# Moving loads, two kv products and the transposes of batch 1 in a fused attention and gated-MLP kernel

## The chip, the cores and the metric

The kernel runs on one core of one Trainium2 chip. The metric is the device time of one execution in microseconds (us). One profiled execution leaves a trace; its span is about 1.8 us shorter than the time of the same execution (285.1 us against 286.9), and span differences equal time differences. The time of one kernel is not one number: 50 runs of the kernel before, over all series, have mean 286.80 us, standard deviation 0.27 us and range 286.39 to 287.32. Effects of a few tenths of a microsecond are read from the trace, and the times only confirm sums.

Ratios are the mean time of one kernel's runs over that of the other's of the same rounds, so not quite the ratio of the medians quoted. An interval is a 95% interval.

## The reference

```python
# q, k, v: (8 batches, 8 heads, 576 tokens, 64), float32
q_s = softmax(q, axis=-1)            # over the 64 of a head
k_s = softmax(k, axis=2)             # over the 576 tokens
kv  = einsum('bhsd,bhse->bhde', k_s, v)
x   = einsum('bhsd,bhde->bhse', q_s, kv)     # -> (4608 tokens, 512)
h   = x @ w_in                        # 512 x 2048
g   = h * sigmoid(beta * h)
out = g @ w_out                       # 2048 x 512
```

## The kernel before

The 4608 tokens are worked in nine slabs `t` of 512 (eight batches, and a ninth slab for the 64 tokens that each batch has over 512, its "remainder"). A slab has two passes of 64 matmuls of 128x512: pass 1 (XT times w_in, then SiLU on ScalarE) and pass 2 (times w_out). The attention of batch t+1 or t+2 is threaded between those matmuls. Heads go in pairs, 0 to 3. For one pair: exp of q on ScalarE, normalization on VectorE or GpSimd, four 128x128 transposes on TensorE; exp of k, nine 65-column matmuls (kv), a scaling of kv on VectorE ("kvd"), one 512-column product that gives the pair's part of XT, and a copy of that from PSUM to SBUF.

A scheduler of its own places them: `(slot, step)`, where the slot counts matmuls of the slab. For slab 0, slots 64 to 128 are pass 2, in which all of batch 1's attention must happen.

```python
def spread(steps, lo, hi):
    return [(lo + (hi - lo) * k / len(steps), s) for k, s in enumerate(steps)]

TT = (116, 128)
...                                    # w_in in five column chunks, cast to bf16 on arrival
for m in (0, 2):
    load_win(0, m, 2)
for c in range(1, len(WCH)):
    load_win(c)
...
for c in range(4):
    load_wout(c)                       # into the same staging buffers
...
# slab 0: what is threaded between the matmuls
todo = [(TT[k_], lambda k_=k_: go(t_steps(1, (2 * k_, 2 * k_ + 1), (1 + k_,)))) for k_ in range(2)]
todo += [(113, lambda: o2_evac(0, 0, 3, ACTE)), (114, lambda: o2_evac(0, 1, 4, ACTE))]
todo.append((114.5, lambda: (exp_kh(1, 2, 2, 0), exp_kh(1, 2, 2, 1))))
todo.append((110, lambda: (norm_main(1, 2, 1), norm_main(1, 3, 1))))
todo += spread(kv_steps(1, (0, 1), (0,)), 121, 122.5)
todo += [(127.5, lambda: (out_now(1, 0, 7, DVE), out_now(1, 1, 1, ACTE)))]
...
for c in range(4):
    scale_wout(c)                      # VectorE: w_out / beta, to bf16
load_main("qf", qt_h, QF, 1, 4)        # batch 1's queries
for cs in ((0, 1), (2, 3)):
    load_k(1, 4, cs)
    load_v(1, 4, cs)
```

Nearly all loads are issued from SyncE's queue, in program order.

The softmax here doesn't subtract the row's maximum and nothing guards it: scores larger than these inputs give would overflow.

Of the kernel before, what the change touches and what calls it, by code (L numbers as in the profile page):

```python
# [158 lines left out]
def bass_efficient_attn_shen__then__act_swish_beta_kernel(  # L159
# [12 lines left out]
    with ExitStack() as es:  # L172
# [74 lines left out]
        def load_main(name, th, bufs, b, split=1, cs=None, engs=(SP,)):  # L247
            i = b % 2
            n = H // split
            for c in cs or range(split):  # L250
                add(engs[c % len(engs)], lambda e, c=c: e.dma_start(dst(bufs[i], c * n, n), src(th, b, c * n, n)),  # L251
                    w=[(name, i, hp) for hp in range(c * n // 2, (c + 1) * n // 2)],
                    slot=f"{name}{i}_{c}")
# [23 lines left out]
        def load(b):  # L277
# [5 lines left out]


        load_main("qf", qt_h, QF, 0, 4, None, (SP, ACTE))
        add(ACTE, lambda e: e.activation(DUMMY[:, 0:1], WARM[:, 0:1], ACT.Exp), r=["warm"],
            w=["dummy"])

# [195 lines left out]
            return s  # L484

        def attn_late(b):
            s = spread(kv_steps(b, (0, 1)), 99, 103) + spread(kv_steps(b, (2, 3)), 105, 109)
            x = []
            for hp in range(NHP):
                x += out_step(b, hp, MB)  # L490
            return s + spread(x, 110, 123)

        def spread(steps, lo, hi):
            return [(lo + (hi - lo) * k / len(steps), s) for k, s in enumerate(steps)]
# [31 lines left out]
        def out_now(b, hp, bk, eng):  # L526
            i = b % 2
            out_mm(b, hp, bk)
            add(eng, lambda e: (e.copy if eng == ACTE else e.tensor_copy)(
                XT[i][:, hp, :], PS[bk][:, :]),  # L530
                r=[("ps", bk)], w=[("xt", i, hp)], bank=[bk])
# [13 lines left out]
                s()  # L545


        for i, n in enumerate((2, 4)):
            a = bass.AP(beta_h, FG[n][0], [[128 * n, len(FG[n])], [1, 128 * n]])
            add(SP, lambda e, i=i, a=a: e.dma_start(BT[i][:, :], a), w=[("bt", i)],  # L550
                slot=f"bt{i}")
        load_k(0, 4)
        load_v(0, 4)

# [20 lines left out]
        def wkeys(c, m, nm):  # L575
            if c == 0:
                return [("wst", 0, h) for h in range(m // 2, (m + nm + 1) // 2)]
            return SKEY[0][2:] if c == 1 else SKEY[c - 1]

        def load_win(c, m=0, nm=NM):  # L580
            c0, n = WCH[c]
            a = bass.AP(win_h, m * 128 * DFF + c0, [[DFF, 128], [128 * DFF, nm], [1, n]])
            s = STAGE[c0 // 512][:, m:m + nm, c0 % 512:c0 % 512 + n]
            add(SP, lambda e: e.dma_start(s, a), w=wkeys(c, m, nm), slot=f"win{c}{m}")  # L584
# [54 lines left out]
        norm_main(0, 3, 1)  # L639
        go(t_steps(0, (1,), HEAD))  # L640
        warm(1, 0, True)
        for m in (0, 2):
            load_win(0, m, 2)
        for c in range(1, len(WCH)):
            load_win(c)
        cast_v(0, 0)
        cast_v(0, 2)
        cast_v(0, 3, POOL, 1)
# [15 lines left out]
        def pass1_mm(t, f, m, bk):  # L664
            x = XT8 if t == 8 else XT[t % 2]
            rd = [("xt8", p_) for p_ in range(4)] if t == 8 else [("xt", t % 2, m)]
            if (t, m) in ((0, 0), (0, 2), (0, 3), (1, 2), (1, 3)):
                rd = rd + [("xh", t, m)]
            n = 2 if f < 8 else 4
            l = bass.AP(WIN, m * DFF + 128 * (f // n * n) + f % n, [[NM * DFF, 128], [n, 128]])  # L670
            mm(PS[bk][:, :], l, x[:, m, :], m == 0, m == NM - 1,
               r=rd + [("win", c, m) for c in range(len(WCH))
                       if WCH[c][0] <= 128 * (f // n * n) < WCH[c][0] + WCH[c][1]],
               w=[("ps", bk)], bk=bk)
            if m == NM - 1:
                add(ACTE, lambda e: e.activation(GT[:, f, :], PS[bk][:, :], ACT.Silu,  # L676
                                                 scale=BETA[:, f:f + 1]),
                    r=[("ps", bk), "beta"], w=[("gt", f)], bank=[bk])
# [18 lines left out]
                tick()  # L697

        FIRST = (2, 5)
        TT = (116, 128)  # L700
        at = first_tiles(0, FIRST[0])
        kv_mm(0, 0, 3, 0)
        kv_mm(0, 1, 3, 1)
        kvd(0, 0, 3, 0, 2)
        kv_mm(0, 2, 5, 0, D + 1)
        out_halves(0, 0, 4, 6)
        kv_mm(0, 3, 5, 1, D + 1)
        out_now(0, 1, 7, ACTE)
        ksum_inv(0, 5, 2, 2, D, VW)
        kvd(0, 2, 5, 0, 2)  # L710
        at(0)
        out_halves(0, 2, 3, 4)
        out_halves(0, 3, 6, 7)
        beta = read_beta()
        next(beta)
        next(beta)
# [8 lines left out]
                cast_win(c, m, 1, DVE)  # L725
        for e_ in range(2):
            homes_ek(1, e_, [("win", 3, NM - 1)])
        for c in range(4):
            load_wout(c)

        def o2_evac(t, u, bk, eng=DVE):
            add(eng, lambda e: (e.copy if eng == ACTE else e.tensor_copy)(  # L732
                O2S[t % 2][:, u, :], PS[bk][:, :]),
                r=[("ps", bk)], w=[("o2", t % 2, u)], bank=[bk])
# [12 lines left out]

        def pass2_group(t, us, bks, tick):
            if t == 0:
                order = [(f, u) for f in range(NF // 2) for u in us]  # L750
                order += [(f, u) for h in (us[0:2], us[2:4]) for f in range(NF // 2, NF) for u in h]
            else:
                order = [(f, u) for f in range(NF) for u in us]
            for f, u in order:
                for bk in (bks[us.index(u)],):
                    mm(PS[bk][:, :], GT[:, f, 128 * u:128 * u + 128], WOUT[:, f, :], f == 0,
                       f == NF - 1, r=[("gt", f), ("wout", f)], w=[("ps", bk)], bk=bk)
                    tick()
            if t == 0:
                return  # L760
            for u, bk in zip(us, bks):
                o2_evac(t, u, bk)
                if t == 8:
                    store8(u)

        for t in range(NSLAB):
            todo = []
            if t == 0:
                todo = [(TT[k_], lambda k_=k_: go(t_steps(1, (2 * k_, 2 * k_ + 1), (1 + k_,))))
                        for k_ in range(2)]  # L770
                todo += [(113, lambda: o2_evac(0, 0, 3, ACTE)), (114, lambda: o2_evac(0, 1, 4, ACTE))]
                todo.append((114.5, lambda: (exp_kh(1, 2, 2, 0), exp_kh(1, 2, 2, 1))))
                todo.append((110, lambda: (norm_main(1, 2, 1), norm_main(1, 3, 1))))
                todo += spread(kv_steps(1, (0, 1), (0,)), 121, 122.5)
                todo += [(127.5, lambda: (out_now(1, 0, 7, DVE), out_now(1, 1, 1, ACTE)))]
            elif t == 1:
                todo = spread(outr_steps(1), 97, 101) + attn_late(2)
            elif t < 7:
                todo = attn(t + 1)
            todo = sorted(todo, key=lambda x: -x[0])  # L780
# [21 lines left out]
            for f in range(FIRST[t] if t < 2 else 0, NF):  # L802
                pass1_tile(t, f, tick)
            if t == 0:
                for c in range(4):
                    scale_wout(c)
                load_main("qf", qt_h, QF, 1, 4)
                for cs in ((0, 1), (2, 3)):
                    load_k(1, 4, cs)
                    load_v(1, 4, cs)  # L810
                load(2)
                load_qrem(0)
                exp_q(1)
                exp_kh(1, 0, 2, 0)
                exp_kh(1, 0, 2, 1)
                for hp in range(2):
                    norm_main(1, hp, 1, POOL if hp == 1 else DVE)
                for hp in range(NHP):
                    cast_v(1, hp)
                pass2_group(0, (0, 1, 2, 3), (3, 4, 5, 6), tick)  # L820
                while todo:
                    todo.pop()[1]()
                at = first_tiles(1, FIRST[1])
                add(ACTE, lambda e: e.activation(DUMMY[:, 2:3], WARM[:, 0:1], ACT.Silu),
                    r=["warm"], w=["dummy"])
                o2_evac(0, 2, 5, DVE)
                at(0, 0, 2)
                go(kv_steps(1, (2, 3), (3,)))
                at(0, 2)
                at(1, 0, 3)  # L830
                out_halves(1, 2, 7, 3)
                at(1, 3)
                out_halves(1, 3, 7, 3)
                at(2)
                at(3)
                o2_evac(0, 3, 6, DVE)
                store(0)
                load(3)
                continue
# [20 lines left out]
            for u in range(4):  # L860
                pass2_group(t, (u,), (OB[orot[0] % 2],), tick)
                orot[0] += 1
                if t == 1 and u == 0:
                    for hp in range(2, 4):
                        norm_main(2, hp, 1, POOL)
                    t_dma(2, 2, 2)
                    for hp in range(NHP):
                        cast_v(3, hp)
                    load(4)
# [34 lines left out]
```

## Time and profile before

| | before |
|---|---|
| median of 3 runs, as known when predicting | 286.99 us (286.59 to 287.23) |
| TensorE busy | 276.7 of 285.1 us |
| distance of 128x512 matmuls, start to start | 0.216 us |
| DMA engines busy | 1.0 or more from about 2.5 to 60 us |

Three lines of the profile page of the kernel before: the span, the busy time by engine, and the busy tenths of the DMA engines in 40 slices of 7.1 us.

```profile
span 285.1 us, 3855 instructions
PE 276.7 (97%) x1548; PEld 135.6 (48%) x1579; DVE 116.1 (41%) x214; ACT 177.1 (62%) x241; POOL 38.2 (13%) x60
...
DMA  7999999995999999207970033002500020021022
```

TensorE sets the time and the DMA engines are full for the first quarter. "Busy" is weak evidence on TensorE, since its matmuls overlap: the Trainium skill, "Perfetto Trace Analysis", says at its head that matmul busy time is a bad metric for this reason, and here the 128x512 matmuls show a mean of 379 ns although they start 216 ns apart. So losses are read from the distance of starts. I call a "wait" the distance from one matmul's start to the next, less 0.218 us for a 512-column one. In some traces, about one matmul record in fifty is missing, which looks like a false wait of 0.214 us; those are left out.

Two places are worth showing. First the weight loads of TensorE near 19 us (timeline of the kernel before; start, duration, engine, line, what is written and read, count, and in brackets the idle time before it and what ended it):

```profile
18.94 0.10 PEld L365 LDWEIGHTS PS<-XT,WIN 128*128 128x128 bf16 x1 [0.55 <-DVE WIN L590]
19.27 0.10 PEld L365 LDWEIGHTS PS<-XT,WIN 128*128 128x128 bf16 x1 [0.24 <-DVE WIN L590]
19.61 0.10 PEld L365 LDWEIGHTS PS<-XT,WIN 128*128 128x128 bf16 x1 [0.24 <-DVE WIN L590]
19.95 0.55 PEld L365 LDWEIGHTS PS<-XT,WIN 128*128 128x128 bf16 x4 [0.24 <-DVE WIN L590]
```

Each step waits for one cast of the third w_in chunk, because the chunk has only just landed: 0.57 us in all. Second, the matmuls at batch 1's head, from the kv products (VB,EK) to the first matmul on batch 1's XT:

```profile
42.45 0.19 PE L365 MATMUL PS<-VB,EK 128*128 128x65 bf16 x1
...
43.44 1.24 PE L365 MATMUL PS<-WOUT,GT 128*128 128x512 bf16 x5
44.53 0.39 PE L365 MATMUL PS<-QT,KVD 128*128 128x512 bf16 x1
44.97 0.61 PE L363 MATMUL PS<-IDB,EQ 128*128 128x128 bf16 x8
45.79 0.59 PE L365 MATMUL PS<-XT,WIN 128*128 128x512 bf16 x2 [0.21 <-ACT EK L316]
```

After kv, the scaling runs during matmuls of pass 2, two products (one record missing) give XT of pairs 0 and 1, and part of the copy of XT runs during the transposes. The last line comes 0.37 us late. The bracket names ScalarE, the last semaphore by the profile; the copy on VectorE ended at 45.64, so that is what it waited for.

### The profile page before, as it was taken

How to read it: one execution, taken by the hardware profiler on the slowest of the kernel's cores; microseconds unless marked ns; L12 is line 12 of the kernel's file. 1: busy time of each engine (PE TensorE's matmuls, PEld its weight loads, DVE VectorE, ACT ScalarE, POOL GpSimd, SP SyncE). 2: the span in 40 equal slices, each digit the busy share in tenths (PEclk: the TensorE clock that was granted, in tenths of full speed). 3: DMA queues.
4: the chain of work that ended last, by engine and by line, in shares of the span. 5: the costliest groups of instructions: out<-in, count | busy, mean ns of one | idle time of the engine just before them, and what ended most of it. 6: DMA issues, size and time to landing. Idle time of an engine off the chain costs nothing.

```text
span 285.1 us, 3855 instructions
## 1 busy us (share of the span) xinstructions
PE 276.7 (97%) x1548; PEld 135.6 (48%) x1579; DVE 116.1 (41%) x214; ACT 177.1 (62%) x241; POOL 38.2 (13%) x60
## 2 busy tenths in 40 slices
PE   7999999999999999999999999999999999999994
PEld 3635445445455445544554445444544444444441
DVE  4754697009781248124731473055705200110021
ACT  5788478889977935796479636892650185028400
POOL 6622031306302031200130000000000000000000
PEclk9999999999999999999999999999999999999999
DMA  7999999995999999207970033002500020021022
GB/s 236 375 384 410 387 384 378 343 382 97 266 400 199 382 333 336 60 24 245 382 105 1 2 148 74 2 1 110 131 0 0 37 113 0 0 92 57 0 74 74
DMA packets 41438, 50.07 MB, mean 176 GB/s; under 512 B 20166, under 2 KB 29386, under 8 KB 40140
## 3 DMA queue, kind: packets, MB, share of 16 engines
q1 hardware_dynamic: 40556, 48.77, 53.4%
q10 hardware_dynamic: 864, 1.05, 1.1%
q8 instruction: 12, 0.20, 0.3%
q14 instruction: 6, 0.05, 0.0%
HBM read 36.71 MB, written 9.44 MB: 162 GB/s over the span
## 4 chain that ended last, share of the span: by engine, by line
PE 82%; DMA 8%; SPq 5%; ACT 2%; issue 1%; DVE 1%; ACTq 0%
PE PS L365 82%; DMA O2S<-in_moe_w_in_dram 5%; DMA KF<-in_k_dram 3%; SPq L261 2%; ACT EK L316 2%; SPq L584 1%; SPq L251 1%; DVE WIN L590 0%; DVE O2S L732 0%; ACT GT L676 0%; SPq L550 0%; ACT O2S L732 0%; SPq L563 0%; ACTq L142 0%
## 5 line engine op out<-in xcount | busy, mean ns | idle before, releaser
L676 ACT ACTIVATE GT<-PS,BETA 128x512 bf16<-128x512 f32 x144 | 97.5, 689 | 77.9 <-PE PS L365 77.7
L365 PE MATMUL PS<-XT,WIN 128*128 128x512 bf16 x560 | 131.1, 379 | 0.8 <-ACT EK L316 0.2
L365 PE MATMUL PS<-WOUT,GT 128*128 128x512 bf16 x563 | 131.2, 379 | 0.6
L365 PEld LDWEIGHTS PS<-XT,WIN 128*128 128x128 bf16 x576 | 60.0, 106 | 59.5 <-DVE WIN L590 1.3
L365 PEld LDWEIGHTS PS<-WOUT,GT 128*128 128x128 bf16 x576 | 54.5, 98 | 62.8 <-DVE O2S L732 0.2
L732 DVE COPY O2S<-PS 128x512 f32<-128x512 f32 x34 | 23.3, 686 | 110.7 <-PE PS L365 110.7
L365 PE MATMUL PS<-VB,EK 128*128 128x65 bf16 (+2 forms) x306 | 35.7, 191 | 0.4
L350 POOL CAST VB<-VF 128x576 bf16<-128x576 f32 (+1 forms) x31 | 22.1, 714 | 73.2 <-DMA VF<-in_v_dram 53.7
L306 ACT ACTIVATE EK<-KF 64x1152 bf16<-64x1152 f32 x24 | 27.8, 1158 | 0.4
L365 PEld LDWEIGHTS PS<-VB,EK 128*128 128x128 bf16 x306 | 22.1, 98 | 7.0 <-issue 0.3
L294 ACT ACTIVATE EQ<-QF 128x512 bf16<-128x512 f32 x32 | 17.9, 619 | 5.8 <-DMA QF<-in_q_dram 5.4
L331 DVE TENSOR_REDUCE QS<-EQ 128x8 f32<-128x512 bf16 (+1 forms) x22 | 20.1, 914 | 3.4 <-ACT EQ L294 3.2
L440 DVE CAST XT<-PS 128x512 bf16<-128x512 f32 x24 | 16.5, 691 | 10.9 <-PE PS L365 10.9
L333 DVE TENSOR_TENSOR EQ<-EQ,QI 128x1024 bf16<-128x1024 bf16 (+1 forms) x15 | 16.5, 1098 | 0.5
L365 PE MATMUL PS<-QT,KVD 128*128 128x512 bf16 (+1 forms) x36 | 11.6, 351 | 0.5 <-DVE KVD L402 0.4
L333 POOL TENSOR_TENSOR EQ<-EQ,QI 128x512 bf16<-128x512 bf16 x7 | 7.3, 1043 | 26.3 <-DVE QI L332 26.0
L316 ACT ACTIVATE EK<-KF 64x1152 bf16<-64x1152 f32 (+1 forms) x10 | 9.5, 966 | 1.9 <-DMA KF<-in_k_dram 1.8
L365 PE MATMUL PS<-XT 128*128 128x512 f32 x12 | 7.9, 786 | 1.5 <-DVE XT L221 1.5
L402 DVE TENSOR_TENSOR KVD<-PS,RC 64x128 bf16<-64x128 f32 (+1 forms) x22 | 7.7, 350 | 1.3 <-PE PS L365 0.6
L339 DVE TENSOR_REDUCE QRS<-EQR 128x8 f32<-128x512 bf16 x4 | 2.7, 680 | 13.4 <-ACT EQR L321 13.4
L294 ACT ACT_TABLE_LOAD x5 | 6.4, 1283 | 0.1
L676 ACT ACT_TABLE_LOAD x5 | 6.4, 1283 | 0.1
(53 smaller groups left out, 76.2 us busy)
## 6 DMA issues: line engine op xcount, KB each, us to landing
out_dram<-O2S SPq DMA_DIRECT2D x8, 1024.0 KB, 5.5
KF<-in_k_dram SPq DMA_DIRECT2D x6, 1152.0 KB, 9.2
VF<-in_v_dram SPq DMA_DIRECT2D x6, 1152.0 KB, 12.2
QF<-in_q_dram SPq DMA_DIRECT2D x6, 1024.0 KB, 7.8
KF<-in_k_dram SPq DMA_DIRECT2D x8, 288.0 KB, 7.2
VF<-in_v_dram SPq DMA_DIRECT2D x8, 288.0 KB, 7.4
O2S<-in_moe_w_in_dram SPq DMA_DIRECT2D x2, 1024.0 KB, 13.1
WST<-in_moe_w_out_dram SPq DMA_DIRECT2D x2, 1024.0 KB, 10.4
```

What stands on the lines that cost most here:

```text
L261: add(SP, lambda e, a=a, o=o: e.dma_start(o, a), w=[(name, i, hp) for hp in range(c * n, c * n + n)], slot=f"{name}{i}_{c}")
L294: add(ACTE, lambda e, o=o, a=a: e.activation(o, a, ACT.Exp), r=[("qf", i, hp)], w=[("eq", i, hp)])
L306: add(ACTE, lambda e, o=o, a=a: e.activation(o, a, ACT.Exp), r=[("kf", i, h) for h in hps], w=[("ek", i, h, e_) for h in hps])
L316: add(ACTE, lambda e: e.activation(o, a, ACT.Exp), r=[("kf", i, h) for h in hps], w=[("ek", i, h, e_) for h in hps])
L331: add(DVE, lambda e: e.tensor_reduce(s_, a, AX.X, ALU.add), r=ks, w=[("qs", i, hp0)])
L333: add(eng, lambda e: e.tensor_tensor(a, a, vb, ALU.mult), r=ks + [("qi", i, hp0)], w=ks)
L350: add(eng, lambda e: (e.copy if eng == ACTE else e.tensor_copy)(o, a), r=[("vf", i, hp), ("vone", i)], w=[("vb", i, hp, h) for h in ((0, 1 ...
L365: add(PE, lambda e: e.matmul(o, l, r_, start=start, stop=stop), r=r, w=w, bank=[bk])
L402: add(DVE, lambda e, o=o, a=a, s_=s_: e.tensor_tensor(o, a, s_, ALU.mult), r=[("ps", bk)] + [("rc", i, h) for h in hps], w=[("kvd", i, h, ...
L440: add(eng, lambda e: (e.copy if eng == ACTE else e.tensor_copy)(XT[i][:, hp, :], PS[bk][:, :]), r=[("ps", bk)], w=[("xt", i, hp)], bank=[bk])
L676: add(ACTE, lambda e: e.activation(GT[:, f, :], PS[bk][:, :], ACT.Silu, scale=BETA[:, f:f + 1]), r=[("ps", bk), "beta"], w=[("gt", f)], ba ...
L732: add(eng, lambda e: (e.copy if eng == ACTE else e.tensor_copy)(O2S[t % 2][:, u, :], PS[bk][:, :]), r=[("ps", bk)], w=[("o2", t % 2, u)], ...
```

## The change

Its intent is to fill the waits of the first 46 us: load what is needed first earlier, split a load so that its first half can be cast sooner, move the transposes of batch 1 forward, and hide the products' latencies. The diff, cut to its core:

```diff
+        # beta: on ScalarE's queue instead of SyncE's, ahead of K
+            add(ACTE, lambda e, i=i, a=a: e.dma_start(BT[i][:, :], a), ...)
-        for m in (0, 2):
-            load_win(0, m, 2)
-        for c in range(1, len(WCH)):
-            load_win(c)
+        for c in range(len(WCH)):
+            for m in (0, 2) if c in (0, 2) else (0,):
+                load_win(c, m, 2 if c in (0, 2) else NM)
...
-        TT = (116, 128)
+        TT = (107, 118)
         kv_mm(0, 2, 5, 0, D + 1)
-        out_halves(0, 0, 4, 6)
         kv_mm(0, 3, 5, 1, D + 1)
-        out_now(0, 1, 7, ACTE)
+        out_now(0, 0, 4, ACTE)
+        out_now(0, 1, 6, ACTE)
...
-        for c in range(4):
+        for c in range(3):
             load_wout(c)
+        load_main("qf", qt_h, QF, 1, 4)
+        load_wout(3)
...
-                order = [(f, u) for f in range(NF // 2) for u in us]       # pass 2 of slab 0
+                order = [(f, u) for f in range(12) for u in us]
...
-                todo += [(113, ... o2_evac(0, 0, 3, ACTE)), (114, ... o2_evac(0, 1, 4, ACTE))]
-                todo.append((114.5, lambda: (exp_kh(1, 2, 2, 0), exp_kh(1, 2, 2, 1))))
-                todo.append((110, lambda: (norm_main(1, 2, 1), norm_main(1, 3, 1))))
-                todo += spread(kv_steps(1, (0, 1), (0,)), 121, 122.5)
-                todo += [(127.5, lambda: (out_now(1, 0, 7, DVE), out_now(1, 1, 1, ACTE)))]
+                todo += [(120, ... o2_evac(0, 0, 3, ACTE)), (120, ... o2_evac(0, 1, 4, ACTE))]
+                todo.append((120.5, lambda: (exp_kh(1, 2, 2, 0), exp_kh(1, 2, 2, 1))))
+                todo.append((100, lambda: (norm_main(1, 2, 1), scale_wout(3), norm_main(1, 3, 1))))
+                todo += spread(kv_steps(1, (0, 1), (0,)), 121, 122)
+                todo += [(126, lambda: out_now(1, 0, 7, DVE)), (127, lambda: out_now(1, 1, 1, DVE))]
             elif t == 1:
-                todo = spread(outr_steps(1), 97, 101) + attn_late(2)
+                todo = spread(outr_steps(1), 98.5, 101) + attn_late(2)
...                                       # attn_late: kv 99 -> 101, outputs 110 -> 111
...                                       # kv of pairs 2, 3: behind three matmuls on XT, not two
-                        norm_main(2, hp, 1, POOL)
+                        norm_main(2, hp, 1, POOL if hp == 2 else DVE)
```

More of the change, by code (lines that the diff above doesn't have):

```diff
@@ L285, in bass_efficient_attn_shen__then__act_swish_beta_kernel @@
         load_main("qf", qt_h, QF, 0, 4, None, (SP, ACTE))
+        for i, n in enumerate((2, 4)):
+            a = bass.AP(beta_h, FG[n][0], [[128 * n, len(FG[n])], [1, 128 * n]])
+            add(ACTE, lambda e, i=i, a=a: e.dma_start(BT[i][:, :], a), w=[("bt", i)],
+                slot=f"bt{i}")
         add(ACTE, lambda e: e.activation(DUMMY[:, 0:1], WARM[:, 0:1], ACT.Exp), r=["warm"],
@@ L486, in attn_late @@
         def attn_late(b):
-            s = spread(kv_steps(b, (0, 1)), 99, 103) + spread(kv_steps(b, (2, 3)), 105, 109)
+            s = spread(kv_steps(b, (0, 1)), 101, 104) + spread(kv_steps(b, (2, 3)), 105, 109)
             x = []
@@ L490, in attn_late @@
                 x += out_step(b, hp, MB)
-            return s + spread(x, 110, 123)
+            return s + spread(x, 111, 123)
         def spread(steps, lo, hi):
@@ L545, in go @@
                 s()
-        for i, n in enumerate((2, 4)):
-            a = bass.AP(beta_h, FG[n][0], [[128 * n, len(FG[n])], [1, 128 * n]])
-            add(SP, lambda e, i=i, a=a: e.dma_start(BT[i][:, :], a), w=[("bt", i)],
-                slot=f"bt{i}")
         load_k(0, 4)
@@ L577, in wkeys @@
                 return [("wst", 0, h) for h in range(m // 2, (m + nm + 1) // 2)]
+            if c == 2:
+                return SKEY[1][m // 2:(m + nm + 1) // 2]
             return SKEY[0][2:] if c == 1 else SKEY[c - 1]
@@ L666, in pass1_mm @@
             rd = [("xt8", p_) for p_ in range(4)] if t == 8 else [("xt", t % 2, m)]
-            if (t, m) in ((0, 0), (0, 2), (0, 3), (1, 2), (1, 3)):
+            if (t, m) in ((0, 2), (0, 3), (1, 2), (1, 3)):
                 rd = rd + [("xh", t, m)]
@@ L711, in bass_efficient_attn_shen__then__act_swish_beta_kernel @@
         at(0)
-        out_halves(0, 2, 3, 4)
-        out_halves(0, 3, 6, 7)
+        out_halves(0, 2, 7, 3)
+        out_halves(0, 3, 4, 5)
         beta = read_beta()
@@ L749, in pass2_group @@
             if t == 0:
-                order = [(f, u) for f in range(NF // 2) for u in us]
-                order += [(f, u) for h in (us[0:2], us[2:4]) for f in range(NF // 2, NF) for u in h]
+                order = [(f, u) for f in range(12) for u in us]
+                order += [(f, u) for h in (us[0:2], us[2:4]) for f in range(12, NF) for u in h]
             else:
@@ L770, in bass_efficient_attn_shen__then__act_swish_beta_kernel @@
                         for k_ in range(2)]
-                todo += [(113, lambda: o2_evac(0, 0, 3, ACTE)), (114, lambda: o2_evac(0, 1, 4, ACTE))]
-                todo.append((114.5, lambda: (exp_kh(1, 2, 2, 0), exp_kh(1, 2, 2, 1))))
-                todo.append((110, lambda: (norm_main(1, 2, 1), norm_main(1, 3, 1))))
-                todo += spread(kv_steps(1, (0, 1), (0,)), 121, 122.5)
-                todo += [(127.5, lambda: (out_now(1, 0, 7, DVE), out_now(1, 1, 1, ACTE)))]
+                todo += [(120, lambda: o2_evac(0, 0, 3, ACTE)), (120, lambda: o2_evac(0, 1, 4, ACTE))]
+                todo.append((120.5, lambda: (exp_kh(1, 2, 2, 0), exp_kh(1, 2, 2, 1))))
+                todo.append((100, lambda: (norm_main(1, 2, 1), scale_wout(3), norm_main(1, 3, 1))))
+                todo += spread(kv_steps(1, (0, 1), (0,)), 121, 122)
+                todo += [(126, lambda: out_now(1, 0, 7, DVE)), (127, lambda: out_now(1, 1, 1, DVE))]
             elif t == 1:
-                todo = spread(outr_steps(1), 97, 101) + attn_late(2)
+                todo = spread(outr_steps(1), 98.5, 101) + attn_late(2)
             elif t < 7:
@@ L804, in bass_efficient_attn_shen__then__act_swish_beta_kernel @@
             if t == 0:
-                for c in range(4):
+                for c in range(3):
                     scale_wout(c)
-                load_main("qf", qt_h, QF, 1, 4)
                 for cs in ((0, 1), (2, 3)):
@@ L826, in bass_efficient_attn_shen__then__act_swish_beta_kernel @@
                 o2_evac(0, 2, 5, DVE)
-                at(0, 0, 2)
+                at(0, 0, 3)
                 go(kv_steps(1, (2, 3), (3,)))
-                at(0, 2)
+                at(0, 3)
                 at(1, 0, 3)
```

## The prediction

> **What bounds the kernel now.** TensorE. The page gives it 276.7 us busy of a 285.1 us span at a granted clock of 1.0. In the timeline its 128x512 matmuls start 0.216 us apart almost without a break from 14.5 us to the end; batches 2 to 7 hold nothing to win. The list of what TensorE waited for has only 2.7 us, 1.5 of it at the very start. Reading start-to-start times, I find these recoverable losses: 0.59 us at 13.0 (kv product scaled by VectorE), 0.28 at 14.7, 0.57 at 18.5 to 19.9 (casts of the third w_in chunk), 0.37 at 45.4 (XT of batch 1), 0.14 at 48.5, about 0.25 at 67.7 to 74. Together 2.2 us, 0.8% of the time. No change of order can give 2%.
>
> The second limit is the DMA engines. They are busy (share 1.0 or more) from about 2.5 us past 60 us, at 350 to 420 GB/s. Whatever is reordered there lands later by what is put ahead of it.
>
> **Each step, costed.**
> - Beta on ScalarE's queue: SyncE issues K 0.74 us sooner. The Trainium skill, "DMA: Bandwidth & Descriptors", section "Issuing engines are not separate DMA queues", says this saves only sequencer time. The trace agrees: Q's packets fill the engines until 5.3 us. I expect K to land within 0.15 us of 7.54. Worth nothing.
> - kv of pairs 2, 3 first, XT of pair 0 whole: nine 65-column matmuls (0.28 us) fill the 0.59 us gap, but one 0.59 us ScalarE copy replaces two of 0.4 us in parallel. At most 0.3 us locally.
> - Third chunk in two loads: rows 0, 1 land near 17.1 instead of 18.43, so the 0.57 us stall shrinks by about 0.5. But the fifth chunk still lands near 25.15 and its four casts end at 26.61, where TensorE today needs the last at 26.87. So only about 0.2 us of all start-up gains survives; the first output-projection matmul moves from 29.67 to about 29.4.
> - Queries of batch 1 ahead of the last w_out chunk: each lands about 2.6 us earlier (33.5 to 35.8 instead of 36.1 to 38.4), the chunk about 3 us later (38.4 instead of 35.37). K and V stay (39.1 to 44.4). The new order over 12 blocks puts the need for that chunk at 40.2, so it is in time. But its four scalings (1.7 us of VectorE) now stand before pair 3's normalization, so pair 3's transposes may wait 0 to 0.4 us near 41.7.
> - Transposes earlier, XT copies on VectorE: the chain K, exp (2.35 us), kv, scaling, out, copy still ends batch 1's head; K's landing pins it. The 0.37 us loss may stay, or move.
> - Batch 2's last normalization on VectorE, later steps: removes most of the 0.25 us near 68 to 74.
>
> **On the critical path:** about 0.2 (start) + 0.2 (batch 2) + 0.1 (rest). Predicted 286.4 us, range 285.6 to 287.1. Chances: faster by over 2% 0.01, within 2% 0.98, slower 0.01.
>
> **What the profile would show.** Right: matmuls of the fourth feature block begin without 0.34 us steps near 19; the next bite is at the fifth chunk's casts near 26; Q of batch 1 lands near 33.5; the first kv product of batch 1 is near 42.5, its first matmul on XT within 0.4 us of 45.8; from 80 us on, the same steps shifted.
> Wrong: the fifth chunk landing before 24.8, or the kv product of batch 1 before 42.0; then the gain is nearer 1.2 us.
>
> **What would make it wrong.** A longer wait for pair 3's transposes or for the late w_out chunk (slower, by up to 1 us); one DMA engine's lag, which spreads the landings of one load over 2.4 us, changing with the new order.

## The result

| | before | changed |
|---|---|---|
| median | 286.79 us (4 runs, 286.39 to 287.23) | 287.18 us (4 runs, 286.84 to 287.31) |
| ratio | | 1.0012 (0.9993 to 1.003) |
| second series | 286.65 us (11 runs) | 286.77 us (6 runs, 286.32 to 288.78), 1.0017 (0.9994 to 1.004) |

It is not shown to differ at all: both intervals hold 1. In the second series one run of 288.78 us carries the excess; the mean of the five others is 286.68 us against 286.66 for the kernel before. What is shown is that the forecast gain of about 0.5 us did not come. The profile page of the changed kernel:

```profile
span 285.4 us, 3851 instructions
PE 276.8 (97%) x1547; PEld 135.7 (48%) x1578; DVE 117.8 (41%) x215; ACT 176.6 (62%) x240; POOL 38.1 (13%) x59
...
DMA  7999999995997999207970033002500020021022
```

The page tells the two apart nowhere, so the places shown before must be looked at. The weight loads near 19 us (line numbers are two to four higher in this kernel):

```profile
18.22 1.20 PEld L369 LDWEIGHTS PS<-XT,WIN 128*128 128x128 bf16 x6
19.66 0.81 PEld L369 LDWEIGHTS PS<-XT,WIN 128*128 128x128 bf16 x5 [0.24 <-DVE WIN L592]
```

The steps of 0.34 us are gone (the one remaining bracket costs no matmul its slot). The first matmul of pass 2 comes at 29.45 us instead of 29.67. Then batch 1's head:

```profile
41.56 0.61 PE L367 MATMUL PS<-IDB,EQ 128*128 128x128 bf16 x8
42.00 0.81 PE L369 MATMUL PS<-WOUT,GT 128*128 128x512 bf16 x3
42.65 0.19 PE L369 MATMUL PS<-VB,EK 128*128 128x65 bf16 x1
...
43.65 0.81 PE L369 MATMUL PS<-WOUT,GT 128*128 128x512 bf16 x3
44.55 0.39 PE L369 MATMUL PS<-QT,KVD 128*128 128x512 bf16 x1
...
45.21 0.38 PE L369 MATMUL PS<-WOUT,GT 128*128 128x512 bf16 x1
45.81 0.81 PE L369 MATMUL PS<-XT,WIN 128*128 128x512 bf16 x3 [0.23 <-DVE XT L533]
```

All sixteen transposes now stand before kv, and less stands behind it: four large matmuls up to the product (one record missing) where there were five. The product waits 0.25 us for the scaling (44.08 to 44.55; VectorE ended it at 44.49) and the first matmul on XT waits 0.39 us for the copy: 0.64 us where it was 0.37. It starts at 45.81, as late as before (45.79). Last, near 68 us, the remainder products (QTR) wait for a transposing DMA. The kernel before, then the changed one:

```profile
68.06 0.20 PE L365 MATMUL PS<-QTR,KVD 128*128 128x64 bf16 x1
```

```profile
68.84 0.23 PE L369 MATMUL PS<-QTR,KVD 128*128 128x64 bf16 x2 [0.29 <-DMA QTR<-EQR]
```

By the distance of starts that wait is 0.45 us; in the trace of the kernel before it was 0.17, too short for a bracket (the DMA landed at 68.02). So by these two traces: 0.22 us won at the start (29.67 to 29.45), 0.24 lost from there to the first matmul on XT (16.12 to 16.36), 0.28 lost near 68, and the changed execution is 0.3 us longer (285.4 against 285.1). The experiments ask which of these belong to the change.

### The profile page after: what moved, and what is told of

It is laid out like the page before. It is cut to its first block, busy times and chain, and to the rows that moved or that the text cites. A ratio compares the mean times of both kernels' runs of the same rounds, so it can differ in the third digit from the quotient of the medians. Undisturbed runs are those within 1.5% of the kernel's fastest.

```text
span 285.4 us, 3851 instructions
## 1 busy us (share of the span) xinstructions
PE 276.8 (97%) x1547; PEld 135.7 (48%) x1578; DVE 117.8 (41%) x215; ACT 176.6 (62%) x240; POOL 38.1 (13%) x59
## 4 chain that ended last, share of the span: by engine, by line
PE 89%; DMA 4%; DVE 1%; SPq 1%; issue 1%; ACT 1%; POOL 0%; POOLq 0%
PE PS L369 89%; DMA VF<-in_v_dram 3%; DMA QTR<-EQR 1%; SPq L261 1%; ACT L325 0%; POOL VB L354 0%; PE PS L367 0%; SPq L251 0%; ACT GT L677 0%; DVE XT L533 0%; DVE QRS L343 0%; DVE O2S L735 0%; DVE EQR L346 0%; ACT EQR L325 0%; ACT XT L533 0%
## 5 line engine op out<-in xcount | busy, mean ns | idle before, releaser
L354 POOL CAST VB<-VF 128x576 bf16<-128x576 f32 (+1 forms) x31 | 23.1, 744 | 76.7 <-DMA VF<-in_v_dram 71.7
L337 DVE TENSOR_TENSOR EQ<-EQ,QI 128x1024 bf16<-128x1024 bf16 (+1 forms) x16 | 17.4, 1089 | 0.5
L337 POOL TENSOR_TENSOR EQ<-EQ,QI 128x512 bf16<-128x512 bf16 x6 | 6.3, 1043 | 23.3 <-DVE QI L336 23.0
```

Source lines behind the costliest of these rows:

```text
L337: add(eng, lambda e: e.tensor_tensor(a, a, vb, ALU.mult), r=ks + [("qi", i, hp0)], w=ks)
L354: add(eng, lambda e: (e.copy if eng == ACTE else e.tensor_copy)(o, a), r=[("vf", i, hp), ("vone", i)], w=[("vb", i, hp, h) for h in ((0, 1 ...
```

## The experiments

Sixteen runs, two of them of an unaltered kernel, all with correct outputs. Each series is four runs on one chip beside the kernel before.

### Series 1: halves of the change, and two suspected waits

**start_only**: the kernel before with the start-up half (beta, third chunk in two loads, kv of pairs 2, 3 first, XT of pair 0 whole).

```diff
 # on the kernel before: the hunks of beta, load_win, kv_mm/out_now of batch 0; nothing else
```

> The kernel before with the start-up half of the change alone (beta on ScalarE's queue, third chunk in two loads, kv of pairs 2, 3 first, XT of pair 0 whole). If the start-up is worth what the two profiles show, the first output-projection matmul comes near 29.45 us instead of 29.67 and the kernel gains 0.1 to 0.3 us (ratio 0.999 to 0.9997). Rival, that the start-up is worth nothing or costs: first output-projection matmul at 29.6 or later, ratio 1.000 or more.

286.92 us median against 286.64, ratio 1.0005 (0.9993 to 1.0017). The expected ratio is inside the interval and so is 1. Pass 2 began at 29.09 us in its trace, earlier than expected, but the first remainder product then waited 0.22 us for its DMA (landed at 67.47, product at 67.51).

**rest_only**: the changed kernel with that half undone.

```diff
 # on the changed kernel: the same hunks reversed
```

> The changed kernel with the start-up half undone: queries ahead of the last w_out chunk, transposes and order of batch 1's head, batch 2's small moves. Theory that the loss sits here: slower than the kernel before by 0.3 to 0.6 us (ratio 1.001 to 1.002), with TensorE waiting near 44.3 and 45.5 (together about 0.5 to 0.7 us against 0.37) and near 68 for the transposed remainder queries. Rival, that the loss came from the start-up: ratio 1.000 or less.

286.77 us, ratio 1.0006 (0.9994 to 1.0019). The trace has the two head waits (0.25 and 0.39 us) as in the changed kernel, and no wait at all near 68, so that one does not belong to this half.

**kv_earlier**: the kv products of batch 1 before the second transposes.

```diff
-                todo += spread(kv_steps(1, (0, 1), (0,)), 121, 122)
+                todo += spread(kv_steps(1, (0, 1), (0,)), 117, 117.9)
```

> The changed kernel with the kv products of batch 1's pairs 0, 1 issued before the second set of transposes (ticks 117 to 118 in place of 121 to 122). Theory that only the order of instructions pins batch 1's head: the kv products run near 41.6 instead of 42.7, the waits near 44.3 (0.25 us) and 45.5 (0.39 us) shrink to under 0.3 us together, and the kernel gains about 0.4 to 0.6 us on the changed one (ratio to the kernel before 0.998 to 1.000). Rival, as predicted blind, that K's landing and its 2.35 us of exp pin it: TensorE waits near 41.6 for the exp, nothing is gained (ratio 1.000 to 1.002).

287.96 us, ratio 1.004 (1.0027 to 1.0053): slower. My theory failed here, and the rival that the blind prediction held was right about this place, though it had allowed 1.002 at most. TensorE, then ScalarE, in that trace:

```profile
42.15 0.19 PE L369 MATMUL PS<-VB,EK 128*128 128x65 bf16 x1 [0.80 <-ACT EK L320]
```

```profile
39.65 2.35 ACT L320 ACTIVATE EK<-KF 64x1152 bf16<-64x1152 f32 x2 [3.47 <-DMA KF<-in_k_dram]
44.00 1.07 ACT L735 COPY O2S<-PS 128x512 f32<-128x512 f32 x2 [2.00 <-PE PS L369]
45.10 2.35 ACT L320 ACTIVATE EK<-KF 64x1152 bf16<-64x1152 f32 x2
```

kv waited 0.96 us (start to start) for the exp of K, which cannot start before K lands (39.57 here). And the copies, held by their place in the order, kept the exp of pairs 2, 3 off a free ScalarE for 2.00 us, which cost another 0.59 us at 47. So both limits are there, close together: the exp of K ends at 41.3 to 42.3 us, depending on the run, and the order of the changed kernel asks for it at 42.2 to 42.65.

**qrem_later**: the remainder queries of batches 2, 3 loaded after the first transposing DMA of batch 2, not with batch 3.

```diff
-                load(3)
+                load(3, False)          # without load_qrem(2)
...
                     t_dma(2, 0, 2)
+                    load_qrem(2)
```

> The changed kernel with the remainder queries of batches 2, 3 loaded after the first transposing DMA of batch 2 instead of with batch 3. Theory that the wait near 68.5 is for the transposing DMA of batch 0, 1's remainder queries, which stands behind those loads on the same DMA engines: the wait (0.45 us in the changed kernel) falls to under 0.15 us and the kernel gains 0.3 us on the changed one (ratio to before 0.999 to 1.000). Rival, that the wait comes from the normalization before it or from the order: the wait stays at 0.3 us or more. A later transposing DMA of batch 2 may wait for the moved load and give some of it back near 75.

287.83 us, ratio 1.0049 (1.003 to 1.0068): slower. The wait near 68 was gone, as expected, but the second transposing DMA of batch 2 now stood behind the moved load, and a product near 75 waited 0.99 us for it. Right cause, wrong place for the load.

### Series 2: the changed kernel again, and a retuned head

**after_again**: the changed kernel, unaltered.

> The changed kernel once more, unaltered, for a second trace and a second ratio. Theory: the waits near 44.3 and 45.5 us (0.25 and 0.39 us) are in every trace of it, because the order of instructions makes them; the wait near 68.5 (0.45 us in its first trace) is not, because it hangs on when the transposing DMA lands. Ratio to the kernel before 1.000 to 1.002. Rival, that the 68.5 wait belongs to the change: it is there again with 0.3 us or more.

The times are in the table above. In its trace the head waits are 0.25 and 0.39 us again; the wait near 68 is not there.

**kv_right_after**: kv directly behind the second transposes, nothing else.

```diff
-                todo += spread(kv_steps(1, (0, 1), (0,)), 121, 122)
+                todo += spread(kv_steps(1, (0, 1), (0,)), 118.1, 119)
```

> The changed kernel with the kv products of batch 1's pairs 0, 1 right after the second set of transposes (ticks 118.1 to 119) and nothing else. Theory: the exps of K end at 41.3 to 42.0, so the products need not wait; the 0.25 us wait near 44.3 goes (the scaling on VectorE has eight matmuls to hide behind), the 0.39 us wait for the copy of XT stays, because its product still stands at the end of the group. Gain on the changed kernel 0.2 to 0.3 us. Rival, that K's landing pins the head: the 0.25 us comes back as a wait before the kv products, no gain.

287.07 us against 286.65, ratio 1.0014 (1.0002 to 1.0026). The 0.25 us wait went and the 0.39 us one stayed, as expected. But most of the 0.25 us came back ahead of kv: the transposes of pair 3 waited 0.15 us for their normalized queries, and kv 0.06, so the head is only 0.05 us shorter. And the exp of pairs 2, 3 still ran behind ScalarE's copies and ended at 46.57, so the next kv products waited 0.59 us. No gain: a wait taken away alone uncovers the next.

**head_tuned**: the two output products earlier as well, and half of that exp ahead of the copies.

```diff
-                todo += spread(kv_steps(1, (0, 1), (0,)), 121, 122)
-                todo.append((120.5, lambda: (exp_kh(1, 2, 2, 0), exp_kh(1, 2, 2, 1))))
-                todo += [(126, lambda: out_now(1, 0, 7, DVE)), (127, lambda: out_now(1, 1, 1, DVE))]
+                todo += spread(kv_steps(1, (0, 1), (0,)), 118.1, 119)
+                todo += [(119.5, lambda: exp_kh(1, 2, 2, 0)), (120.5, lambda: exp_kh(1, 2, 2, 1))]
+                todo += [(123.2, lambda: out_now(1, 0, 7, DVE)), (124.2, lambda: out_now(1, 1, 1, DVE))]
```

> As the run before it, and also the two output products of batch 1 at ticks 123.2 and 124.2 instead of 126 and 127, and half of the exp of pairs 2, 3 ahead of ScalarE's two copies. Theory: both waits near 44.3 and 45.5 go, the first matmul on batch 1's XT comes near 45.2 instead of 45.8, a gain of 0.5 to 0.65 us on the changed kernel, ratio to the kernel before 0.998 to 1.000. Rival, that the copies or exps on ScalarE or K's landing only move the wait: first matmul on XT at 45.6 or later, or a new wait before the kv products of pairs 2, 3.

286.2 us against 286.65, ratio 0.9985 (0.9973 to 0.9997): faster than the kernel before, and in the same series the changed kernel had 1.0017. Its head on TensorE:

```profile
41.91 0.73 PE L369 MATMUL PS<-VB,EK 128*128 128x65 bf16 x18
42.48 1.24 PE L369 MATMUL PS<-WOUT,GT 128*128 128x512 bf16 x5
43.58 0.39 PE L369 MATMUL PS<-QT,KVD 128*128 128x512 bf16 x1
43.81 0.38 PE L369 MATMUL PS<-WOUT,GT 128*128 128x512 bf16 x1
44.02 0.38 PE L369 MATMUL PS<-QT,KVD 128*128 128x512 bf16 x1
44.24 0.81 PE L369 MATMUL PS<-WOUT,GT 128*128 128x512 bf16 x3
44.89 0.81 PE L369 MATMUL PS<-XT,WIN 128*128 128x512 bf16 x3
45.86 0.73 PE L369 MATMUL PS<-VB,EK 128*128 128x65 bf16 x18 [0.16 <-ACT EK L320]
```

The same matmuls, in another order: five behind kv hide the scaling, four behind the first product hide the copy. The first matmul on XT starts at 44.89 without a wait for the copy (earlier, at 41.42, pair 3's transposes waited 0.14 us); 0.32 us of wait (start to start) comes back at the next kv, where the exp ends late. In the four other traces with this head that last wait is 0, 0, 0.15 and 0.27 us, so it too is partly a draw.

**head_qrem**: head_tuned, with the remainder queries loaded behind *both* transposing DMAs of batch 2.

```diff
                     t_dma(2, 2, 2)
+                    load_qrem(2)
+                    exp_qr(1)
```

> As head_tuned, with the remainder queries of batches 2, 3 loaded after both transposing DMAs of batch 2, and their exp after K's. Theory: nothing waits near 68 for the transposed remainder queries in any run, and unlike qrem_later no transposing DMA of batch 2 stands behind the moved load, so no wait near 74 to 75; as fast as head_tuned or up to 0.3 us faster, ratio to before 0.997 to 0.9995, and a narrower spread of its runs. Rival: the moved load or the later exp delays batch 3 and costs 0.3 us or more.

286.23 us, ratio 0.9985 (0.9973 to 0.9997), as fast as head_tuned. The remainder's transposing DMA landed at 66.91 us, the earliest of all traces, and its product followed without a wait at 67.43. The edit has a price of its own, read in series 4.

### Series 3: the kernel before again, and parts undone in the retuned kernel

**before_again**: the kernel before, unaltered.

> The kernel before, unaltered, for a second trace: ratio 1.000 within 0.1%. The waits made by the order of instructions (0.59 near 13, the 0.34 us steps near 19, 0.37 near 45.4) should be there again; the landing of the last DMA engine (K of pair 1 at 39.87 in its first trace) and the wait near 67.7 may differ by some tenths of a us, as lots drawn anew in each run.

Ratio 1.000 (0.9986 to 1.0014). Its trace is the most instructive of all. Pass 2 began at 28.99 us, not 29.67: the third chunk landed at 17.75 instead of 18.43, and the steps near 19 us, which I had expected to be there again, were not. Batch 1's head came 0.70 us earlier, with its 0.37 us wait. And then:

```profile
68.03 0.20 PE L365 MATMUL PS<-QTR,KVD 128*128 128x64 bf16 x1 [0.69 <-DMA QTR<-EQR]
```

The wait is 0.85 us by the starts: the transposing DMA was issued at 64.59 us, 0.72 us earlier than in the first trace, and landed at 67.99, as it had there (68.02). It stands behind the loads of batch 3 on the same engines. The early arrival was swallowed.

**tuned_old_start**: head_tuned with the start-up half undone.

```diff
 # on head_tuned: the hunks of start_only reversed
```

> The retuned head (head_tuned) with the start-up half of the change undone. If the start-up half is worth about 0.2 us, as the blind prediction had it, this is 0.1 to 0.4 us slower than head_tuned (ratio to before 0.9990 to 0.9998 against 0.9985). Rival, that the start-up is worth nothing once the rest is in order: same ratio, 0.998 to 0.9988.

286.79 us against 286.96, ratio 0.9993 (0.9979 to 1.0008), against 0.9985 for head_tuned. In the expected direction, with intervals that overlap: not settled.

**tuned_q_late**: head_tuned with batch 1's queries behind the last w_out chunk again.

```diff
-        load_main("qf", qt_h, QF, 1, 4)
         load_wout(3)
+        load_main("qf", qt_h, QF, 1, 4)
```

> head_tuned with batch 1's queries loaded behind the last w_out chunk again, as in the kernel before, and nothing else. Theory: the early queries are what lets the transposes stand at 38.6 and 41.5 us. Late, they land at 36.1 to 38.4, the second pair's normalized query is ready near 40.6, so TensorE waits some 1.5 to 2.5 us near 38.6 and the kernel loses 1 to 2.5 us. Rival, that the order of these loads does not matter: within 0.3 us of head_tuned.

289.04 us, ratio 1.0078 (1.0063 to 1.0093), 2.1 us slower than the kernel before by the medians. The transposes wait for the late queries, twice:

```profile
39.93 0.40 PE L367 MATMUL PS<-IDB,EQ 128*128 128x128 bf16 x4 [1.19 <-POOL EQ L337]
...
44.43 0.40 PE L367 MATMUL PS<-IDB,EQ 128*128 128x128 bf16 x4 [1.08 <-DVE EQ L337]
```

The early transposes need the early queries.

**tuned_old_tail**: head_tuned with batch 2's small moves undone.

```diff
-                todo = spread(outr_steps(1), 98.5, 101) + attn_late(2)
+                todo = spread(outr_steps(1), 97, 101) + attn_late(2)
...
-            s = spread(kv_steps(b, (0, 1)), 101, 104) + ...
+            s = spread(kv_steps(b, (0, 1)), 99, 103) + ...
-            return s + spread(x, 111, 123)
+            return s + spread(x, 110, 123)
-                        norm_main(2, hp, 1, POOL if hp == 2 else DVE)
+                        norm_main(2, hp, 1, POOL)
```

> head_tuned with batch 2's small moves undone (remainder products at tick 97, kv at 99, pair 3's normalization on GpSimd). The blind prediction gave them 0.2 us. If so: 0.1 to 0.4 us slower than head_tuned, with waits of 0.2 to 0.5 us between 67 and 75. Rival, that they are worth nothing: same ratio as head_tuned (0.998 to 0.999).

286.65 us against 286.96, ratio 0.999 (0.9977 to 1.0004): not settled. Its trace shows something else. The fourth w_in chunk landed at 22.23 us instead of about 20.9, its casts came late, and TensorE waited 0.99 us near 22:

```profile
22.25 1.43 DVE L592 CAST WIN<-O2S 128x512 bf16<-128x512 f32 x4 [3.34 <-DMA O2S<-in_moe_w_in_dram]
```

Pass 2 began at 30.14 us. That is a lot drawn by the DMA, not the tail.

### Series 4: without the landing near 68

If that landing swallows early arrivals, a start-up gain cannot be seen until it is away. So the moved load of head_qrem went alone into the kernel before (**before_qrem**), its start-up half (**start_qrem**) and the changed kernel (**after_qrem**), beside **head_qrem_again**. The edit is that of head_qrem:

```diff
-                load(3)
+                load(3, False)          # without load_qrem(2)
...
                     t_dma(2, 2, 2)
+                    load_qrem(2)
+                    exp_qr(1)           # and no longer ahead of batch 3's exps of k
```

> The kernel before with only the remainder queries of batches 2, 3 loaded behind both transposing DMAs of batch 2. Theory that the landing near 68.0 absorbs early arrivals: no wait before the first remainder product, gain of 0.2 to 0.6 us, ratio 0.998 to 0.9993. Rival, that the wait of 0.85 us in one trace was an accident: ratio 0.9995 to 1.0005.

> The same in the kernel with the start-up half alone. If the start-up half is worth the 0.2 us predicted, it is 0.1 to 0.4 us faster than before_qrem. Rival, worth nothing: within 0.1 us of before_qrem, or slower.

> The same in the changed kernel. The head's waits (0.25 and 0.39 us against 0.37 in the kernel before) stay in the trace, so it should be 0.2 to 0.3 us slower than start_qrem, and 0.3 to 0.7 us slower than the retuned kernel. Rival, that the loss of the changed kernel came from the remainder queries: as fast as start_qrem.

> head_qrem once more, for a comparison on one chip with the other three: ratio to the kernel before 0.9975 to 0.999 as in its first series; the fastest of the four by 0.2 us or more if the head is where the changed kernel loses.

| | median us | ratio to before (287.05 us, 11 runs) |
|---|---|---|
| before_qrem | 286.66 | 0.9994 (0.9982 to 1.0007) |
| start_qrem | 286.62 | 0.9986 (0.9974 to 0.9998) |
| after_qrem | 286.67 | 0.9992 (0.9980 to 1.0004) |
| head_qrem_again | 286.35 | 0.9983 (0.9971 to 0.9995) |

All four traces are free of the wait near 68. But the moved exp now runs last before ScalarE's next table load (in the kernel before it ran ahead of the exps of k, at 72.40). ScalarE in the trace of before_qrem:

```profile
76.80 0.63 ACT L321 ACTIVATE EQR<-QRF 128x512 bf16<-128x512 f32 x1
77.45 1.28 ACT L676 ACT_TABLE_LOAD   x1
78.74 2.63 ACT L676 ACTIVATE GT<-PS,BETA 128x512 bf16<-128x512 f32 x4
```

TensorE waits 0.23 us for the first of these SiLUs near 79, in all five traces with this edit; in the twelve traces with the remainder's load and exp unmoved it waits 0 to 0.10 us there. So the edit takes one wait away and adds another, and the ratios hold both.

The order of the four is the expected one, but the differences (0.2, 0.2 and 0.3 us by the ratios) are within the intervals of each. before_qrem lies between its forecast (0.9993 at most) and the rival's (0.9995 at least), and head_qrem_again is 0.1 us ahead of start_qrem where 0.2 or more was expected. head_qrem has now beaten the kernel before twice, by 0.15 and 0.17%, each time with 1 outside the interval.

### What the eighteen traces say together

The two traces of the first comparison and the sixteen experiments. "Pass 2" is the start of its first matmul, "head" the time from there to the first matmul on batch 1's XT, "landed" the transposed remainder queries.

| trace | third, fourth chunk landed | pass 2 | head | landed | wait there |
|---|---|---|---|---|---|
| before | 18.43, 21.14 | 29.67 | 16.12 | 68.02 | 0.17 |
| before_again | 17.75, 20.46 | 28.99 | 16.10 | 67.99 | 0.85 |
| before_qrem | 17.91, 20.63 | 29.36 | 16.10 | 67.50 | 0 |
| start_only | 18.45, 21.16 | 29.09 | 16.10 (first record on XT missing, 0.216 taken off) | 67.47 | 0.22 |
| start_qrem | 18.13, 22.06 | 29.98 | 16.10 | 68.08 | 0 |
| changed | 18.82, 21.54 | 29.45 | 16.36 | 68.80 | 0.45 |
| after_again | 18.40, 21.12 | 29.03 | 16.36 | 67.64 | 0 |
| after_qrem | 18.29, 21.00 | 28.97 | 16.36 | 67.38 | 0 |
| qrem_later | 18.17, 20.89 | 29.36 | 16.36 | 67.77 | 0 |
| rest_only | 18.16, 20.87 | 29.40 | 16.36 | 68.22 | 0 |
| kv_right_after | 17.99, 20.70 | 29.16 | 16.31 | 68.39 | 0 |
| head_tuned | 17.91, 20.62 | 28.96 | 15.93 | 67.88 | 0.14 |
| head_qrem | 18.26, 20.96 | 28.95 | 15.76 | 66.91 | 0 |
| head_qrem_again | 17.87, 20.58 | 29.35 | 15.76 | 67.15 | 0 |
| tuned_old_start | 18.10, 20.81 | 29.34 | 15.76 | 67.92 | 0.02 |
| tuned_old_tail | 18.13, 22.23 | 30.14 | 15.76 | 67.99 | 0 |

(kv_earlier, head 17.05, and tuned_q_late, head 18.79, wait in the head itself.)

The head's length goes with the order of instructions: 16.10 to 16.12 in five traces with the old order, 16.36 in five with the changed one, 15.76 in four of the five with the retuned one (15.93 in head_tuned, where pair 3's transposes waited). The same holds up to the next product, some 2.3 us on, with the same 64 + 8 large matmuls in every trace: 18.39 to 18.41 us from the start of pass 2 with the old order, 18.69 to 18.70 with the changed one. With the retuned one it is 18.09 to 18.58, because the exp of pairs 2, 3 is late in some runs. So the changed order costs 0.3 us in every trace; the retuned one gains 0.3 us at best and 0.13 in the mean of its five traces, less than the 0.43 us by which head_tuned beats the kernel before. What the rest of that gain is, these runs do not show.

The other columns are drawn anew each run, and not by the DMA alone. Full speed of TensorE begins, by the trace's record of the granted clock, at 4.4 to 6.4 us in fourteen traces and at 7.1 to 7.6 in four (before_qrem, kv_earlier, qrem_later, head_qrem_again); in these four the first kv product of batch 0 starts at 11.52 to 11.57 us instead of 11.02 to 11.29, and pass 2 at 29.30 to 29.36. So one trace of each kernel can settle the old and the changed head, and cannot settle the start or the landing near 68.

## Why the prediction was wrong

The prediction was 286.4 us with a range to 287.1; the median was 287.18. The class (within 2%) was right. Point by point:

- **What bounds it**: right. TensorE's busy time did not move (276.7 and 276.8 us) and the DMA engines stayed full.
- **Beta**: right that it is worth nothing; K of pair 0 landed at 7.71 us against 7.54 (0.02 us outside the 0.15 that I gave), though it was issued 0.74 us sooner. The trace agrees with the section of the Trainium skill that the prediction names. Over all traces K of pair 0 landed at 6.63 to 7.71 us with the new place of beta (thirteen) and at 6.81 to 7.54 with the old (five).
- **kv of pairs 2, 3 first, XT whole ("at most 0.3 us locally")**: not there. In the changed kernel's trace the first matmul on XT came at 15.18 us instead of 14.53. It waited 0.71 us for the whole copy, and in that trace the kv products ahead of it waited 0.41 and 0.31 us for the casts of V. In the other twelve traces with this order the waits between 12.3 and 15.6 us add up to 1.07 to 1.14 us, and to 1.05 to 1.09 in the five with the old one: one wait took the place of another.
- **Third chunk in two loads**: right that the 0.34 us steps go: none of the thirteen traces with the new start has them, and three of the five with the old one do (0.35 to 0.58 us of wait). In ten of the thirteen traces with the new start pass 2 began between 28.95 and 29.36; in the five with the old one between 28.99 and 29.67. In two of the new ones (29.98, 30.14) it began later because the fourth chunk landed late. The means are 29.29 and 29.35. The third chunk's worth, 0.2 us in the prediction, is compatible with every series and shown by none.
- **"But the fifth chunk still lands near 25.15 and its four casts end at 26.61"**: the landing was wrong, the end right by accident. It landed at 24.20, below the 24.8 that I had named as a sign of a larger gain. The first cast then took three times the usual:

```profile
L592 DVE CAST WIN<-O2S x4: 406/414/1337, 24.2 to 26.2; 128x512 bf16<-128x512 f32 x4
```

```profile
23.11 2.17 POOL L238 MEMSET EK<- 64x1152 f32 x2 [6.32 <-DVE WIN L592]
```

  The cast ran from 24.23 to 25.57, GpSimd's second memset from 24.23 to 25.28. The Trainium skill, "SBUF — State Buffer", section "SBUF: two separate sides", says that a VectorE instruction in a two-port mode and a GpSimd instruction contend for one shared port pair, an exclusive lock: the one that starts first has it for the whole instruction, and the other is blocked. Eight traces agree: wherever this cast began well before the memset's end, it ended 0.28 to 0.29 us after it, whether it took 0.54 or 1.34 us; in the other ten it took 0.43. In which mode the cast ran no trace tells.
- **Queries earlier**: right in kind and more: they landed at 32.68 to 34.81 us, the w_out chunk at 37.37. The feared wait of pair 3's transposes did not come in the changed kernel; in kv_right_after and head_tuned it did (0.15 and 0.14 us).
- **"The 0.37 us loss may stay, or move", summed as part of "+ 0.1 (rest)"**: this is the step that failed, a mis-sized term. The head did not gain 0.1 us; it lost 0.26 (16.10 to 16.36), in every trace with that order. I had said that K's landing pins it. In the changed kernel the exp of K ended at 41.31 and kv started at 42.65, so the order pinned it. K's landing is only the next limit (0.96 us of wait in kv_earlier). What I left out was the count of matmuls that stand between dependent steps. Eight transposes (0.44 us) that had stood behind the products, and hid part of the copy, went ahead of kv. Two large matmuls (0.43 us) took their place there, so the wait for the copy stayed (0.37 and 0.39 us); but of the five large matmuls that had hidden the scaling behind kv four were left, and that showed as the new wait of 0.25 us. With five and four large matmuls in these two places (head_tuned) both waits are gone.
- **Batch 2's moves ("removes most of the 0.25 us")**: not shown. The wait near 68 is set by when a transposing DMA lands behind other loads, 67.5 to 68.8 us with those loads in place. It took 0 to 0.85 us in the traces with the old order of batch 2 and 0 to 0.45 in those with the new, which asks for that product 0.43 us later; with those loads in place, one of four old ones and five of eight new ones are free of it. So the moves may have helped as predicted, but the landing is drawn too, and tuned_old_tail (no wait) does not settle it. The wait is 0 in all five traces with the load of the remainder queries behind both transposing DMAs. Apart from it, the stage from 60 to 77 us takes 16.05 us in fifteen of the eighteen traces, with the moves and without.

The sum was loose too: 0.2 + 0.2 + 0.1 from 286.99 is 286.5, and that base was the median of three runs, 0.2 us above the mean of the fifty. With the head at -0.26 us in place of +0.1 and batch 2 at 0, the same sum gives a loss of 0.06 us (start worth 0.2) to 0.26 us (start worth nothing), which the measured ratios allow.

What stays open: the worth of the start-up half by itself, and of batch 2's moves. Their sizes are below what five rounds separate from draws of 0.27 us.

## What to carry to other kernels

When instructions are moved forward because their data is now early, look at what they were hiding where they stood: count the work left between each dependent pair (product, scaling, product, copy, first use) in the new order. An early arrival at one stage is worth its time only if nothing later is pinned to a landing, so follow the gain stage by stage to the next fixed time. And with several traces of one kernel, ask of each interval whether it repeats: here the one that repeated to 0.02 us belonged to the order, and those that varied by 0.7 us to what is drawn anew in each run, the landings of the DMA and the time at which the full clock was granted.

## What the Trainium skill lacked or had wrong

- "DMA: Bandwidth & Descriptors", section "Why a DMA increments its semaphore by 16 and not by 1", has that the engines of one DMA finish independently. It lacks how far apart they drift under a full queue: in these runs the first and the sixteenth part of one load landed 0.4 to 1.6 us apart for the third w_in chunk and 1.5 to 2.4 us apart for the fifth, and the last decides. No page says what makes it grow. In seventeen of eighteen traces it grows by 0.5 to 1.4 us from one chunk to the next, about when one 16 KB packet of the queue that the profile calls "instruction" runs (it starts at 19.5 to 20.9 us and takes 1.1 us); in the changed kernel's trace it did not grow (1.60 and 1.53 us). In the two traces where already the fourth chunk landed late the packet ran earliest, at 19.54 us (at 19.59, in after_again, that chunk was in time). That it is the cause was not tested.
- No page has the run-to-run spread of a kernel like this: 0.27 us of standard deviation at 287 us, and for the start of one stage 28.95 to 30.14 us.
- "DMA: Bandwidth & Descriptors", section "DMA Transpose (X-bar)", gives the constraints of a transposing DMA and not how long a small one takes, alone or behind ordinary loads: the one near 65 us landed 2.48 to 2.53 us after its issue in the six traces with the remainder's load moved behind it, and 2.53 to 3.43 in the twelve with that load ahead of it.
